# One fused attention, gating and MLP kernel: the ninth and tenth heads' q and k loads are tied to earlier heads' maxima

## The chip, the cores and the metric

The kernel runs on one core of a Trainium2 chip. The metric is the device time of one execution in microseconds (us). Lower is better.

## The reference

Four batches of eight heads (576 positions, 64 values per head) go through causal attention with a bias that comes from a running sum of `s`; its output goes through a causal convolution gate and two matrices, and then through a token mixing of rank 32 and a two-layer MLP with a residual. Cut to what matters:

```python
scores = scale * q @ k.T
bias   = -(cum[:, :, :, None] - cum[:, :, None, :])      # cum: running sum of max(s, 0)
scores = where(causal, -1e9, scores + minimum(bias, 0))
attn   = softmax(scores)                                 # row maximum, exp, row sum
x      = attn @ v                                        # heads side by side: (4, 576, 512)
gate   = sigmoid(causal 5-tap convolution of x)
x      = (gate * (x @ w_val)) @ w_out
u      = x + (x.T @ U @ V).T
out    = u + relu(u @ w_ch1) @ w_ch2
```

## The kernel before

The 32 heads (numbered 0 to 31 here, so the ninth and tenth heads are heads 8 and 9) go through one loop, `for n in range(NH + 1)`. Phase `n` of the loop writes down the scores of head `n` (`score`), the transposes of head `n - 1` (`trans`), and after each odd head the products with v for the pair (`attn_v`, `norm`). Work of the dense stages (`dense_work`) and the preparation of weights (`widen`, through `side_step`) is woven in between. From phase 8 on a finished batch's dense work is available; after the loop the rest of it and the MLP (`ch1`, `ch2`) follow.

The code doesn't fix the order in which an engine executes. Every instruction is written down with a priority (its place in the program, moved ahead by the number in `PLAN`, through the helper `Via`), and the framework plays all of them through a simulated timeline with `schedule_with_timeline_sim=True`. An instruction that has a free engine and its inputs in that timeline is placed, even if it stands many phases later in the program. The result is one fixed order per engine, in which each engine then runs: an instruction that waits holds back what stands behind it on that engine. All DMAs of this kernel are issued by SP, so SP's queue too is one such order.

Heads in `WHOLE` (0 to 7, 16 and 30) load q and k straight into the operands `Q1` and `K1`, with four extra rows that carry the bias. The other heads are split into two parts whose products sum up to more precision. For them:

- `load_raw(n)` (L276 to L282) is called two phases ahead, in phase `n - 2`. It takes a buffer with the tag `qk` (two buffers), and SP loads q into partitions 0 to 63 (L281) and k into 64 to 127 (L282). Heads 8 and 9 are the first two heads that use this tag.
- `load_head(n)` (L284) runs one phase ahead and takes `Q1` and `K1` (two buffers each) and `nm` (two buffers), the small tile in which column `c` holds the negated maxima of block `c` of the head's scores, with a sixth column for the first half of the last block. The two extra loads at L297 bring the bias rows.
- `prep_head(n)` (L304) is deferred in phase `n - 1`: `qk_hi` on ACT rounds the loaded tile into `hi`; `qk_lo` on POOL writes the remainder into `Q2`; then SP issues five copies from SBUF to SBUF: `hi` into `Q1`, `K1` and `K2` (`high`), then the remainder from `Q2` into `K2`, and last `hi` into the lower half of `Q2` (`low`). The last one overwrites what the fourth reads, so it waits until the fourth has landed. `hi`, `Q2` and `K2` have two buffers each.
- `score(n, c)` (L474) multiplies `Q1` with `K1` and `Q2` with `K2`, and DVE takes the maxima into `nm` with the same instruction that adds the mask (tag `max`). ACT then takes the exponential (`exp`), PE transposes the result (`trans`), and ACT or DVE copies it out of PSUM into `PTA` and `PTB`.

A phase's order of the blocks is one of two lists, where T is a transpose, S a score and A a product with v:

```python
ORDER0 = "T0 S0 T1 T4 S1 T3 T2 S2 S3 S4"
ORDER = "T0 T1 S0 T2 T3 S1 S2 S3 T4 S4 A0 A1"
```

`fill` adds two small matmuls of no use ahead of every group of transposes up to phase 8; in the rows they are `pt<-causal`. The entry `pace` of `PLAN` belongs to a copy in `wait_for_pace` that `PACED = False` leaves out, so in the kernel before nothing uses it. Since all instructions go through `Via`, nearly all rows below carry L132, the line of that helper; the names of the tiles tell them apart.

Of the kernel before, what the change touches and what calls it, by code (L numbers as in the profile page):

```python
# [20 lines left out]


PLAN = {
    "pace": ("gpsimd", -500),
    "qk_hi": ("scalar", 6000),
    "qk_lo": ("gpsimd", 2000),
    "put": ("sync", 3000),
# [69 lines left out]
def fused_kernel(ctx, tc, qT, kT, vP, s, wval, wout, convw, U, V, w1, w2, rows01, out):  # L97
    nc = tc.nc
    B, H, D, S = qT.shape
# [172 lines left out]
    hd = {}  # L272

    raw = {}

    def load_raw(n):  # L276

        if n < NH and n not in WHOLE:
            b, h = divmod(n, H)
            raw[n] = at.tile([P, S], F32, tag="qk", name="qk")  # L280
            nc.sync.dma_start(raw[n][0:64, :], qT[b, h])  # L281
            nc.sync.dma_start(raw[n][64:, :], kT[b, h])  # L282

# [140 lines left out]
    pace = []  # L424
# [327 lines left out]
    for n in range(NH + 1):  # L752
# [3 lines left out]
        if 2 <= n + 1 < NH:  # L756
            load_head(n + 1, n == 1)
        load_raw(n + 2)
        if n == 1:
            nc.sync.dma_start(craw.bitcast(U32), words(convw))  # L760
# [240 lines left out]
```

## Time and profile before

| | us |
|---|---|
| median of 3 runs | 765.65 |
| lowest, highest of them | 765.28, 770.79 |
| the profiled execution, its own time | 764.93 |
| its span from the first to the last instruction | 762.8 |
| PE busy, share of the span | 743.7, 98% |
| PE weight loads busy, share | 624.8, 82% |
| DVE, ACT, POOL busy | 464.4, 299.2, 291.2 |

The span is what the trace covers; 2.1 us lie around it. The engines are PE (matmul), PEld (its weight loads), DVE, ACT, POOL and SP, which only issues DMAs here. Times in rows count from the start of the span. A busy PE isn't PE at its peak, since the ends of matmuls are modelled.

### The profile page before, as it was taken

How to read it: one execution, taken by the hardware profiler on the slowest of the kernel's cores; microseconds unless marked ns; L12 is line 12 of the kernel's file. 1: busy time of each engine (PE TensorE's matmuls, PEld its weight loads, DVE VectorE, ACT ScalarE, POOL GpSimd, SP SyncE). 2: the span in 40 equal slices, each digit the busy share in tenths (PEclk: the TensorE clock that was granted, in tenths of full speed). 3: DMA queues.
4: the chain of work that ended last, by engine and by line, in shares of the span. 5: the costliest groups of instructions: out<-in, count | busy, mean ns of one | idle time of the engine just before them, and what ended most of it. 6: DMA issues, size and time to landing. Idle time of an engine off the chain costs nothing.

```text
span 762.8 us, 12349 instructions
## 1 busy us (share of the span) xinstructions
PE 743.7 (98%) x4453; PEld 624.8 (82%) x4453; DVE 464.4 (61%) x1052; ACT 299.2 (39%) x785; POOL 291.2 (38%) x321
## 2 busy tenths in 40 slices
PE   8999999899999999999899999999999999999998
PEld 4777888788887998798788888888888888888887
DVE  6798875887657755666749996424582234223234
ACT  4777756875677776633212211111121011001110
POOL 3466754553522233557197765102540024100000
PEclk9999999999999999999999999999999999999999
DMA  5734544644455432021103221100120000000023
GB/s 147 229 120 120 140 118 114 174 119 127 120 124 134 122 100 56 18 85 55 56 1 111 83 87 53 54 1 28 55 85 1 0 28 1 1 0 1 1 111 138
DMA packets 27012, 59.40 MB, mean 78 GB/s; under 512 B 4654, under 2 KB 5294, under 8 KB 26952
## 3 DMA queue, kind: packets, MB, share of 16 engines
q1 hardware_dynamic: 26952, 58.62, 26.9%
q8 instruction: 35, 0.57, 0.3%
q14 instruction: 25, 0.20, 0.1%
HBM read 37.04 MB, written 5.31 MB: 56 GB/s over the span
## 4 chain that ended last, share of the span: by engine, by line
PE 85%; DMA 4%; DVE 4%; ACT 3%; issue 2%; SPq 1%; POOL 0%; ACTq 0%; DVEq 0%
PE d L132 39%; PE acc L132 26%; PE pt L132 8%; PE av L132 6%; PE sc L132 6%; DMA qk<-in_kT 2%; DMA K<-Q 1%; DVE av L604 1%; ACT P L132 1%; DVE P L132 1%; DMA Q<-hi 1%; DVE uT L132 1%; DMA uT<-in_w 0%; ACT PTB L132 0%; ACT hi L132 0%
## 5 line engine op out<-in xcount | busy, mean ns | idle before, releaser
L132 PE MATMUL d<-u,w1h 128*128 128x512 f32 (+1 forms) x640 | 184.2, 371 | 0.0
L132 DVE SCALAR_TENSOR_TENSOR hl<-d,hh 128x512 fp32r<-128x512 f32 (+1 forms) x80 | 50.7, 635 | 170.3 <-ACT hh L861 170.3
L861 ACT ACTIVATE hh<-d 128x512 fp32r<-128x512 f32 (+1 forms) x80 | 44.2, 554 | 274.6 <-PE acc L132 149.5
L132 PEld LDWEIGHTS d<-u,w1h 128*128 128x128 f32 x640 | 116.0, 188 | 22.2
L132 PE MATMUL d<-u,w1l 128*128 128x512 f32 (+1 forms) x320 | 118.6, 371 | 0.0
L132 PE MATMUL acc<-hl,w2h 128*128 128x512 f32 (+1 forms) x320 | 105.0, 371 | 0.0
L132 PE MATMUL acc<-hh,w2h 128*128 128x512 f32 (+1 forms) x320 | 104.4, 372 | 0.5 <-DVE uT L132 0.5
L132 PE MATMUL acc<-hh,w2l 128*128 128x512 f32 (+1 forms) x320 | 102.0, 371 | 0.0
L132 ACT ACTIVATE P<-P,nm 64x64 f32<-64x64 f32 (+4 forms) x160 | 89.0, 560 | 25.2 <-DVE nm L132 24.6
L132 PE MATMUL sc<-K,Q 68*128 68x288 f32 (+11 forms) x384 | 89.1, 344 | 4.6 <-ACT PTB L132 1.8
L132 DVE CUSTOM_DVE_ANT_0 P<-sc,causal 64x64 f32<-64x64 f32 (+4 forms) x160 | 65.2, 421 | 30.8 <-PE sc L132 28.2
L132 PE MATMUL pt<-ident,P 128*128 128x128 f32 x480 | 78.5, 284 | 5.4 <-ACT PTA L139 2.6
L132 DVE TENSOR_TENSOR uT<-acc,uT 128x512 f32<-128x512 f32 (+1 forms) x120 | 70.1, 630 | 22.3 <-PE acc L132 22.2
L132 PEld LDWEIGHTS sc<-K,Q 68*128 68x128 f32 (+2 forms) x384 | 62.2, 193 | 13.2 <-ACT PTB L132 2.6
L132 PEld LDWEIGHTS d<-u,w1l 128*128 128x128 f32 x320 | 60.2, 188 | 11.0
L132 PEld LDWEIGHTS acc<-hh,w2h 128*128 128x128 f32 x320 | 58.7, 188 | 12.1 <-issue 0.9
L132 PEld LDWEIGHTS acc<-hl,w2h 128*128 128x128 f32 x320 | 58.8, 188 | 11.2
L132 PEld LDWEIGHTS acc<-hh,w2l 128*128 128x128 f32 x320 | 58.6, 188 | 11.3
L132 PEld LDWEIGHTS pt<-ident,P 128*128 128x128 f32 x480 | 56.3, 145 | 12.3 <-ACT PTA L139 3.6
L604 DVE SCALAR_TENSOR_TENSOR av<-X,cw,av 128x576 f32<-128x576 f32 x64 | 52.3, 817 | 4.9 <-ACT av L132 4.5
L132 DVE SCALAR_TENSOR_TENSOR scr<-raw,scr 128x512 uint32<-128x512 uint32 (+1 forms) x56 | 52.4, 936 | 1.4
L132 DVE TENSOR_SCALAR scr<-scr 128x512 uint32<-128x512 uint32 x56 | 43.3, 773 | 11.9 <-POOL w1l L132 6.3
(123 smaller groups left out, 1286.9 us busy)
## 6 DMA issues: line engine op xcount, KB each, us to landing
raw<-in_w SPq DMA_DIRECT2D x28, 512.0 KB
K<-hi SPq DMA_DIRECT2D x44, 144.0 KB
Q<-hi SPq DMA_DIRECT2D x44, 144.0 KB
V<-in_vP SPq DMA_DIRECT2D x16, 320.0 KB
out<-uT SPq DMA_DIRECT2D x16, 256.0 KB
qk<-in_qT SPq DMA_DIRECT2D x22, 144.0 KB
qk<-in_kT SPq DMA_DIRECT2D x22, 144.0 KB
K<-Q SPq DMA_DIRECT2D x22, 144.0 KB
```

The source lines that it names most:

```text
L132: return f(*args, **kw)
L604: Via("tap").scalar_tensor_tensor(g, X[:, k:k + S], cw[:, p, k:k + 1], g, op0=ALU.mult, op1=ALU.add,)
L861: Via("hh").activation(h_, o, AF.Relu)
```

## The change

Ahead of the two loads of heads 8 and 9 a copy of one column, by POOL, is put into the first column of the tile that is about to be loaded. Its source is column 4 of `nm` of the head three before: head 5 for head 8, head 6 for head 9. Column 4 is the last of that head's maxima. The loads overwrite that column, so the framework lets them wait for the copy, and the copy for the maxima. The values computed are the same. `pace` gets a 0 in place of -500, so that the copy keeps its place in the program as its priority.

```diff
 PLAN = {
-    "pace": ("gpsimd", -500),
+    "pace": ("gpsimd", 0),
...
             raw[n] = at.tile([P, S], F32, tag="qk", name="qk")
+            if H <= n < H + 2:
+
+                Via("pace").tensor_copy(raw[n][:, 0:1], hd[n - 3]["nm"][:, 4:5])
             nc.sync.dma_start(raw[n][0:64, :], qT[b, h])
             nc.sync.dma_start(raw[n][64:, :], kT[b, h])
```

## Rows read from the trace of the kernel before

**Rows 1.** The page's part 1: busy time, share of the span and instructions.

```profile
PE 743.7 (98%) x4453; PEld 624.8 (82%) x4453; DVE 464.4 (61%) x1052; ACT 299.2 (39%) x785; POOL 291.2 (38%) x321
```

**Rows 2.** Windows: stretch, its length, busy time per engine, PE clock, DMA share, GB/s.

```profile
12.00:16.00 4.00, 3.53 (x16) 3.02 (x17) 0.59 (x4) 2.46 (x10) 0.26 (x1) 0.57 0.93 218
16.00:17.00 1.00, 1.00 (x12) 0.98 (x11) 0.00 (x0) 0.97 (x3) 0.00 (x0) 1.00 0.92 260
23.00:57.00 34.00, 34.00 (x252) 25.78 (x252) 30.07 (x92) 26.49 (x80) 19.56 (x22) 1.00 0.57 169
57.00:70.00 13.00, 12.64 (x98) 9.70 (x95) 9.94 (x24) 8.66 (x26) 9.44 (x9) 1.00 0.42 131
90.00:130.00 40.00, 37.92 (x288) 33.93 (x289) 26.88 (x83) 25.59 (x74) 20.38 (x27) 0.96 0.46 116
130.00:323.00 193.00, 186.61 (x1419) 161.48 (x1419) 140.31 (x418) 137.28 (x397) 79.89 (x89) 0.99 0.43 108
```

**Rows 3.** The timeline of PE: start, duration, operation; in brackets idle before and releaser.

```profile
12.47 0.60 PE L132 MATMUL sc<-K,Q 68*128 68x64 f32 x2 [0.98 <-DVE nm L132]
...
22.47 0.66 PE L132 MATMUL pt<-ident,P 128*128 128x128 f32 x4 [0.69 <-ACT P L132]
...
66.37 2.53 PE L132 MATMUL sc<-K,Q 68*128 68x320 f32 x8 [0.17 <-ACT PTA L132]
...
69.42 0.39 PE L132 MATMUL sc<-K,Q 68*128 68x64 f32 x2
70.17 0.38 PE L132 MATMUL pt<-causal 128*128 128x256 bf16 x2 [0.36 <-DVE nm L132]
...
76.95 0.41 PE L132 MATMUL sc<-K,Q 68*128 68x64 f32 x2
```

**Rows 4.** The timeline of SP, the queue that issues the DMAs.

```profile
4.99 0.47 SPq L281 DMA_DIRECT2D qk<-in_qT  x1
5.50 0.59 SPq L282 DMA_DIRECT2D qk<-in_kT  x1
...
17.00 0.50 SPq L132 DMA_DIRECT2D Q<-hi  x1
...
18.21 0.49 SPq L282 DMA_DIRECT2D qk<-in_kT  x1
```

**Rows 5.** The timeline of ACT, the `hi` of heads 9 and 10.

```profile
21.08 0.68 ACT L132 ACTIVATE hi<-qk 128x576 fp32r<-128x576 f32 x1 [1.72 <-DMA qk<-in_kT]
...
65.04 0.69 ACT L132 ACTIVATE hi<-qk 128x576 fp32r<-128x576 f32 x1 [3.19 <-DMA Q<-hi]
```

**Rows 6.** The tile `qk`: instructions, count, duration least/median/most in ns, first and last start.

```profile
L132 ACT ACTIVATE hi<-qk x22: 665/684/690, 10.1 to 271.5; 128x576 fp32r<-128x576 f32 x22
L132 POOL TENSOR_TENSOR Q<-qk,hi x22: 1402/1430/1902, 10.9 to 284.0; 128x576 fp32r<-128x576 f32 x22
```

**Rows 7.** The timeline of DVE, the last maxima of heads 5 and 6.

```profile
54.57 0.09 DVE L132 DVE_READ_ACCUMULATOR2_ANT nm<- 128x1 f32 x1
...
60.04 0.08 DVE L132 DVE_READ_ACCUMULATOR2_ANT nm<- 128x1 f32 x1
```

**Rows 8.** The timeline of POOL.

```profile
23.33 0.20 POOL L365 TENSOR_SCALAR uT<-uT 128x20 f32<-128x20 f32 x1
...
55.94 0.62 POOL L132 TENSOR_SCALAR wvh<-uT 128x512 fp32r<-128x512 f32 x1 [2.53 <-DVE uT L132]
...
59.00 1.27 POOL L132 TENSOR_TENSOR wvl<-uT 128x512 fp32r<-128x512 f32 x1 [0.69 <-DVE rs L132]
```

**Rows 9.** The chain of waits: start, duration, what; DMAs from issue to landing.

```profile
12.81 4.17 DMA K<-Q
...
59.47 4.74 DMA Q<-hi
...
127.25 3.40 DMA qk<-in_kT
...
170.89 2.31 DMA K<-Q
...
239.96 1.99 DMA qk<-in_kT
```

## The prediction, made before the changed kernel ran

> **What bounds the kernel now.** I read the busy shares first, then windows by stage, then the chain of waits, and then the timelines of PE, SP, ACT, POOL and DVE around the places where the chain leaves PE. PE is busy for 98% of the span [rows 1], so what a change can give is PE idle time, or time at a low clock. The windows show where that is. From 23 to 57 us PE has no idle time at all [rows 2]: whatever comes out of the stretch before 23 us is carried through, and whatever is added on another engine there costs nothing as long as PE's inputs arrive. Before it stands a start-up with PE idle time and with four microseconds at a mean granted clock of 0.57 [rows 2], between the levels of 1.2 and 2.4 GHz. From 57 to 70 us PE is idle for 0.36 us of 13, and from 90 to 323 us for (40 - 37.92) + (193 - 186.61) = 8.47 us [rows 2].
>
> The chain of waits is the third thing to see. Between 12.8 and 22.5 us it doesn't run through PE at all, but through work of heads 8 and 9, which PE needs only at 69.42 and 76.95 us (their first scores) [rows 3]. Their loads stand at 5 us in SP's order, since nothing holds them back [rows 4], and the scheduler has placed `hi`, `lo` and three of the five copies of each behind them. The last copy of head 8 stands at 17.00 us in SP's order because it waits for the fourth, which takes 4.17 us to land [rows 4, 9]; head 9's load of k, behind it in SP's order, starts at 18.21 us [rows 4]; ACT, whose next instruction is head 9's `hi`, stands still for 1.72 us until that lands [rows 5]; an exponential behind it comes late, and PE idles for 0.69 us ahead of its transposes at 22.47 us [rows 3].
>
> A second such place is at 65 us: ACT stands still for 3.19 us, since head 10's `hi` has to wait until head 8's copy of `hi` into `Q1`, issued at 59.47 us, has landed 4.74 us later [rows 5, 9]. PE loses 0.17 and 0.36 us behind it [rows 3].
>
> **The change part by part.**
>
> *The two copies.* The trace has no POOL copy of one column. Its nearest small row on POOL is 128 x 20 in 0.20 us [rows 8]; I take that, twice, and nothing as the lower bound. Head 5's last maxima are there at 54.57 + 0.09 = 54.66 us, head 6's at 60.04 + 0.08 = 60.12 us [rows 7]. At the first of these times POOL is idle (2.53 us ahead of 55.94), at the second it is in an instruction until 60.27 [rows 8]. The cover is that idle time; without it, the copy would hold back weight preparation by 0.2 us, which no chain here ends in. Cost: 0.
>
> *What leaves the start.* Two `hi` of 0.68 us on ACT, two `lo` of 1.43 us on POOL [rows 6], four loads, six copies, and the loads of heads 10 and 11, which follow in the freed buffers. PE gets back the 0.69 us at 22.47 us, and carries it to about 65 us, as PE has no idle time in which it could be lost [rows 2, 3]. Gain: 0.69, bounds 0.3 and 0.69. The slow clock from 12 to 16 us costs 4 x (1 - 0.57) = 1.72 us of PE time [rows 2]. It follows on a PE that idled 0.98 us ahead of head 1's first scores at 12.47 us, and a little before that [rows 3]; these wait for the cumulated bias, not for head 8. So I take 0 of it, and keep 0 and 1.72 as bounds.
>
> *Where it goes.* Into 55 to 75 us. POOL there gets 2 x 1.43 + 2 x 0.20 = 3.3 us onto the 9.44 of 13 us that it is busy, ACT 1.4 us onto 8.66, and the DMA engines ten transfers of 147 KB, 1.47 MB, which over 13 us are 113 GB/s onto 131 [rows 2, 6]. That is 244 GB/s, where the trace has 218 at a share of 0.93 in the crowded stretch from 12 to 16 us [rows 2]. So everything fits, and nothing has much room.
>
> *Head 8, just in time or late.* From 54.66 us: copy 0.20, first issue 0.47, and from 55.4 us on the load of k, which lands after 1.99 to 3.40 us [rows 4, 9], so at 57.4 to 58.8. `hi` 0.69 and `lo` 1.43 [rows 6], the latter behind up to 1.27 us of other POOL work [rows 8]: 59.5 to 62.2. The fourth copy takes 2.31 to 4.17 us [rows 9]: 61.8 to 66.4. The fifth, which waits for it, takes as much as the fourth at best and 4.74 us at most [rows 9]: 64.1 to 71.1. PE asks at 69.42 [rows 3], or at 68.7 if the 0.69 us is carried. So head 8 is 4.6 us early or 2.4 us late; the middle, 67.6, is early, so I take 0, with 2.4 us as the upper bound.
>
> What the trace says of such a transfer: 4.17 and 4.74 us in crowded stretches, 2.31 in a quiet one [rows 9]. The Trainium skill, "DMA: Bandwidth & Descriptors", section "Anatomy of one DMA — SWDGE (gpsimd) path", gives a fit, for POOL-issued DMAs, of about 2.0 us plus the bytes at 436 GB/s; as an estimate from that page 147 KB would take 2.3 us each. By that, head 8 is ready at about 65 us and never late; by the crowded rows it is late. The two rows in question are twice the fit, so this case's crowded stretches don't agree with it.
>
> *Head 9* waits for 60.12 us. The same terms (POOL in its instruction until 60.27, then copy, load, `hi`, `lo`, two copies in a row) give 70.2 to 77.2 us against 76.95 - 0.69 = 76.3. But its loads share SP with head 8's fifth copy, which holds SP until head 8's fourth has landed, 66.4 us at the latest. In the worst order head 9 is 5.9 us later still, so 6.9 us late.
>
> *The stall at 65 us* (0.53 us of PE): head 10's `hi` still waits for copies of head 8's `hi`, now later, and head 9's `hi` joins it. I take it as moved, not removed: 0, bounds -0.53 and +0.7 (one more stall of the size of that at 22.47 us).
>
> **Sum.** 764.93 (the profiled execution's own time) - 0.69 + 0 + 0 + 0 = 764.2. That execution is 0.72 below the median of the runs, so in terms of the median: 764.9. With the bounds of the small terms the likeliest case alone lies between 763 and 766.5.
>
> **The rivals.**
>
> *A, late operands (slower).* Heads 8 and 9 miss PE's order. Price: up to 2.4 us for head 8 and 6.9 for head 9, and for each such idle time a stretch at half clock like that from 12 to 16 us, 1.72 us; at most 12.7 us, 777.6. The middle, head 8 late by 1.2 us with one slow stretch, gives 764.9 + 2.9 = 767.8. It decides against the change as soon as the lateness is over 0.69 us, and by over 1% only if head 9's loads fall behind head 8's fifth copy on SP. For it: SP's order is one, the transfers of 4.17 and 4.74 us [rows 9]. Against: the scheduler knows of these waits and can put other matmuls ahead of those scores. The clock is part of this price. The trace has it at 0.57 after PE had idled [rows 2, 3]; the Trainium skill, "TensorE: Matmul & The Clock Gate", section "HAM oscillation — how this bites in real kernels", says the same of a PE that waits for a DMA: it falls back to the half clock and does the work behind the wait cold. On that the trace agrees.
>
> *B, the whole start comes free.* The slow clock goes too, and the stall at 65 us: 764.9 - 1.72 - 0.53 = 762.7. For it: six copies and two loads fewer in the stretch of 0.93 DMA share [rows 2]. Against: head 1's scores don't wait for them.
>
> *C, another order later on.* The schedule is played through anew, and shifts of a microsecond at 20 to 75 us can change which instruction comes first for the rest of the attention. At stake is the idle time from 90 to 323 us, 8.47 us: gone, 756.4; doubled, 773.4. Nothing in the trace says which.
>
> *D, no stall at stake:* PE's 0.69 us comes back as another wait before 65 us. Then 765.65, inside the likeliest case's own range.
>
> **How the numbers follow.** The likeliest case with D 0.48; A 0.27, of which 0.10 beyond 1%; B 0.12; C 0.13, of which 0.07 over 1% faster and 0.03 over 1% slower. One per cent, 7.7 us, is about what a measurement of this kernel can tell from no change. So faster 0.07, slower 0.13, same 0.80. The range leaves out most of C's faster part and the far end of A and of C's slower part, together below 0.2: 760.0 to 770.5.
>
> **What would show it.** Right: no `hi` on ACT before 55 us, SP's first load of `qk` at about 55 us, PE without idle time at 22 us, head 1's first scores unmoved at about 12.5 us, head 5's last maxima about 0.7 us earlier. Wrong, for A: PE waiting on `K<-Q`, `Q<-hi` or the first two-part scores between 65 and 80 us, or a granted clock below 1 there. For B: a clock of 1 from 12 to 16 us. For C: stages up to 90 us alike and the difference behind them. What would make the forecast wrong most easily is SP's order around 60 us.

## The result and the profile after

The changed kernel is slower by about half a per cent. Its median is 772.64 us (770.87 to 775.61, 18 runs); the kernel before, run beside it, has 767.44 us (764.36 to 772.53, 18 runs). The ratio is 1.0058 with a 95% interval of 1.0038 to 1.0078 (it isn't the quotient of the two medians, which is 1.0068). The prediction was 764.9 us, within 760.0 and 770.5: the time lies above that range, and the sign is the other one. The size is within the 1% that the prediction called "same". The profiled execution of the changed kernel took 772.69 us, 7.8 us more than that of before, so the two traces differ by more than the medians do (5.2 us).

The first part of the page shows that the work has stayed what it was [rows 1]: 2 more instructions on POOL, the copies, and busy times within 1% of before. The added time is time in which PE waits or runs slowly.

```profile
PE 745.4 (97%) x4453; PEld 626.8 (81%) x4453; DVE 461.5 (60%) x1052; ACT 299.1 (39%) x785; POOL 291.1 (38%) x323
```

Windows of the kernel after, with the columns of [rows 2] (stretch, length, busy time of PE, PEld, DVE, ACT and POOL, granted PE clock, DMA share, GB/s):

```profile
12.00:20.00 8.00, 6.43 (x29) 5.79 (x30) 0.59 (x4) 3.67 (x13) 0.00 (x0) 0.57 0.63 179
20.00:57.00 37.00, 36.74 (x270) 28.63 (x269) 29.48 (x94) 27.59 (x82) 18.70 (x21) 1.00 0.41 128
57.00:70.00 13.00, 13.00 (x97) 9.53 (x96) 9.81 (x28) 9.06 (x27) 8.53 (x10) 1.00 0.55 137
70.00:90.00 20.00, 16.51 (x124) 14.12 (x123) 14.11 (x43) 13.57 (x40) 11.79 (x11) 0.91 0.71 188
90.00:130.00 40.00, 37.46 (x289) 33.11 (x289) 32.16 (x89) 26.97 (x78) 22.74 (x26) 1.00 0.52 124
130.00:150.00 20.00, 19.13 (x156) 16.88 (x152) 14.23 (x45) 15.13 (x45) 10.82 (x14) 1.00 0.54 144
150.00:160.00 10.00, 7.59 (x55) 6.43 (x53) 9.97 (x31) 8.99 (x26) 6.25 (x8) 1.00 0.66 171
160.00:310.00 150.00, 145.58 (x1114) 127.60 (x1115) 101.46 (x319) 103.93 (x305) 56.12 (x64) 1.00 0.46 113
310.00:330.00 20.00, 18.53 (x131) 14.76 (x131) 13.47 (x36) 12.02 (x32) 10.75 (x11) 0.91 0.06 17
```

The same windows of the kernel before, without the two that [rows 2] has already:

```profile
12.00:20.00 8.00, 7.53 (x40) 6.14 (x41) 2.13 (x11) 5.26 (x17) 0.26 (x1) 0.79 0.75 182
20.00:57.00 37.00, 36.31 (x270) 27.75 (x270) 30.80 (x96) 28.41 (x85) 20.72 (x22) 1.00 0.59 177
...
70.00:90.00 20.00, 19.51 (x154) 16.65 (x153) 18.75 (x56) 16.18 (x47) 14.03 (x13) 1.00 0.60 150
...
130.00:150.00 20.00, 19.80 (x153) 16.96 (x151) 16.87 (x50) 17.37 (x49) 11.12 (x13) 1.00 0.54 142
150.00:160.00 10.00, 7.83 (x44) 6.04 (x44) 9.13 (x26) 6.90 (x21) 4.22 (x6) 0.83 0.49 120
160.00:310.00 150.00, 147.44 (x1143) 129.51 (x1143) 103.66 (x318) 104.98 (x308) 55.79 (x64) 1.00 0.44 112
310.00:330.00 20.00, 18.53 (x141) 15.84 (x140) 14.70 (x33) 9.79 (x26) 12.77 (x12) 1.00 0.08 27
```

Lost PE time in a window can be counted as its length less PE's busy time, plus its length times one less the clock. From 12 to 20 us that is 0.47 + 8 x 0.21 = 2.15 us before and 1.57 + 8 x 0.43 = 5.01 after. All windows in that way:

| stretch, us | lost before | lost after | difference |
|---|---|---|---|
| 12 to 20 | 2.15 | 5.01 | +2.86 |
| 20 to 57 | 0.69 | 0.26 | -0.43 |
| 57 to 70 | 0.36 | 0.00 | -0.36 |
| 70 to 90 | 0.49 | 5.29 | +4.80 |
| 90 to 130 | 3.68 | 2.54 | -1.14 |
| 130 to 160 | 4.07 | 3.28 | -0.79 |
| 160 to 310 | 2.56 | 4.42 | +1.86 |
| 310 to 330 | 1.47 | 3.27 | +1.80 |

The sum is +8.6 for a span that is 7.9 us longer. The same work doesn't stand in the same window in both, and idle time at a low clock is counted twice (0.7 us of the 5.01), so each entry is good to about a microsecond. Two entries are the largest: the start and the stretch from 70 to 90 us. In between the change gives what it was to give, the idle time at 22 us and at 65 us. A large part of the entry at the start will turn out to belong to the one execution and not to the kernel (e2 and e16 below).

**The start.** SP's order of the kernel before (start, duration, line, operation), with the stores `ef<-uT` of bias rows behind both of head 1's loads of bias rows:

```profile
9.57 0.69 SPq L297 DMA_DIRECT2D K<-uT  x1
10.37 0.61 SPq L297 DMA_DIRECT2D Q<-uT  x1
...
11.65 1.06 SPq L341 DMA_DIRECT2D ef<-uT  x2
```

SP's order of the kernel after:

```profile
9.56 0.69 SPq L300 DMA_DIRECT2D K<-uT  x1
10.30 0.43 SPq L344 DMA_DIRECT2D ef<-uT  x1
10.84 0.63 SPq L300 DMA_DIRECT2D Q<-uT  x1
...
56.54 0.47 SPq L284 DMA_DIRECT2D qk<-in_qT  x1
...
65.68 0.46 SPq L132 DMA_DIRECT2D Q<-hi  x1
66.19 0.60 SPq L285 DMA_DIRECT2D qk<-in_kT  x1
...
68.28 0.59 SPq L285 DMA_DIRECT2D qk<-in_kT  x1
```

One store has moved ahead of head 1's second load, which is issued 0.47 us later; from there to head 1's first scores it takes 2.73 us and not 2.10. The timeline of PE after, with idle time and releaser in brackets, shows head 1's first scores at 13.57 us and not at 12.47 [rows 3]:

```profile
13.57 0.66 PE L132 MATMUL sc<-K,Q 68*128 68x64 f32 x2 [2.66 <-issue]
...
71.56 0.39 PE L132 MATMUL sc<-K,Q 68*128 68x64 f32 x2
74.48 0.52 PE L132 MATMUL pt<-causal 128*128 128x256 bf16 x2 [2.53 <-ACT PTA L139]
```

**The stall at 72 us.** The last row of that timeline is the largest single wait of PE between 20 and 90 us, and its releaser is ACT. The timeline of ACT after:

```profile
73.09 0.68 ACT L132 ACTIVATE hi<-qk 128x576 fp32r<-128x576 f32 x1 [1.94 <-DMA qk<-in_kT]
73.68 0.55 ACT L132 ACTIVATE P<-P,nm 128x320 f32<-128x320 f32 x1
74.22 0.20 ACT L139 ACTIVATE PTA<-pt 128x64 f32<-128x64 f32 x1
```

ACT stands in front of head 10's `hi` until that head's load of k, issued at 68.28 us, has landed. Behind it in ACT's order are an exponential of head 7 and the copy out of PSUM that PE needs. PE idles for 2.53 us and then works at a reduced clock: the window from 70 to 90 us has 0.91 in the mean.

### The profile page after: what moved, and what is told of

The parts are those of the page before. It is cut to its first block, busy times and chain, and to the rows that moved or that the text cites. A ratio compares the mean times of both kernels' runs of the same rounds, so it can differ in the third digit from the quotient of the medians.

```text
span 770.7 us, 12346 instructions
## 1 busy us (share of the span) xinstructions
PE 745.4 (97%) x4453; PEld 626.8 (81%) x4453; DVE 461.5 (60%) x1052; ACT 299.1 (39%) x785; POOL 291.1 (38%) x323
## 4 chain that ended last, share of the span: by engine, by line
PE 80%; DMA 6%; DVE 5%; ACT 3%; issue 2%; SPq 2%; POOL 1%; ACTq 0%; POOLq 0%; DVEq 0%
PE d L132 37%; PE acc L132 26%; PE pt L132 7%; PE av L132 5%; PE sc L132 5%; DMA qk<-in_kT 3%; DMA K<-Q 2%; DVE av L607 2%; DVE P L132 1%; SPq L132 1%; DVE uT L132 1%; ACT P L132 1%; POOL Q L132 1%; ACT hi L132 1%; DMA Q<-hi 1%
```

## The experiments

Each kernel was compared with the kernel before on the same chip; a ratio is to that kernel, with its 95% interval. The diffs are against the kernel after. Beside the times, the traces were compared by one event: the start of each head's first maxima on DVE, against the same event of before. The shifts, in us:

| kernel | head 1 | 2 | 8 | 9 | 10 | 17 | 31 | ratio |
|---|---|---|---|---|---|---|---|---|
| after | +1.16 | +2.56 | +2.34 | +4.93 | +6.74 | +6.26 | +6.29 | 1.0058 |
| store held (e1) | +0.05 | +1.51 | +1.34 | +3.72 | +5.09 | +9.03 | +8.81 | 1.0035 |
| two heads earlier (e4) | +0.90 | +1.10 | +1.89 | +0.50 | +4.04 | +0.76 | +2.40 | 1.0016 |
| head 10 too (e5) | +1.14 | +2.57 | +2.22 | +0.48 | +2.04 | +6.84 | +6.22 | 0.9982 |
| warm (e7) | +2.32 | +0.92 | -0.14 | +2.30 | +4.17 | +4.91 | +6.49 | 1.0054 |
| only head 8 (e2) | +1.15 | +1.08 | +0.88 | +4.14 | +6.92 | +6.07 | +6.35 | 1.0078 |
| only head 9 (e3) | +1.16 | +2.10 | +1.31 | -0.36 | +6.03 | +6.63 | +7.31 | 1.0086 |
| e5 and e1 (e11) | -0.21 | +0.16 | -0.12 | -1.79 | -0.31 | +0.90 | +0.60 | 0.9997 |
| only head 10 (e13) | +0.05 | +1.09 | -0.51 | -1.28 | -0.48 | +0.98 | +1.18 | 0.9970 |
| `hi` of head 10 on POOL (e16) | +0.89 | +1.10 | +1.09 | +0.17 | +6.05 | +4.70 | +4.66 | 1.0074 |
| only heads 10, 11 (e17) | -0.21 | -0.01 | -0.86 | -1.63 | -1.08 | -1.27 | -1.59 | 0.9978 |

A shift is of one execution, the ratio of many: the execution of e5 in the table is the slowest of its ten.

My theory after the two traces was that two things cost the time, a store that slipped ahead of head 1's second load, and ACT standing in front of head 10's `hi`. Its rivals were late operands of heads 8 and 9 (A of the prediction), the half clock at the start by itself, and an order later on that went worse (C).

### The store at the start

e1 puts a write into a tile that the stores read, so that they are placed later.

```diff
     load_head(1, True)
+    nc.gpsimd.memset(F[3][:, 0:1], 1.0)
     for i in range(2):
         nc.sync.dma_start(ef[:, i], EF[i])
```

> The changed kernel with one more POOL memset (a column of ones, written a second time), so that the store of the bias rows that went ahead of head 1's second bias load on SP can only go behind it. Theory S, the start costs: head 1's first scores come at 12.5 us instead of 13.57, PE's stretch at half clock gets shorter, head 2's first maxima come 1.2 to 2.6 us earlier than in the changed kernel, and the time falls by 1.2 to 2.6 us, to about 770 to 771. Rival L, all of the loss is made where heads 8 to 10 are prepared (70 to 80 us): the time stays at 772 to 773, what the start gives being lost there.

769.61 us (765.89 to 773.75, 10 runs) beside 768.01, ratio 1.0035 (1.0012 to 1.0059). SP has its old order again and head 1 is back in its place (+0.05). Up to head 9 the trace keeps 1.0 to 1.2 us of that. So the cause of head 1's delay is shown. That the total gains is not: the intervals of e1 and after overlap, and the trace loses more at 150 to 180 us than it had gained. The stall at 72 us is there as in after: PE idles for 2.34 us ahead of 73.28.

e7 leaves SP's order at the start and puts 18 small matmuls of no use ahead of head 1's first scores, to hold PE's clock up.

```diff
             o = ps[:, 0:k1 - k0]
+            if n == 1 and c == 0:
+                fill(ps, 18)
             if n in WHOLE:
```

> The changed kernel with 18 more small matmuls of no use ahead of head 1's first scores, in the time in which PE idles from 10.9 to 13.6 us. Theory C, half of what the start costs is the half clock that follows on this idle time (13.4 to 19.9 us in the changed kernel): the granted clock stays at 1 from 12 to 20 us, head 2's first maxima come about 3 us earlier, and the time falls by 2 to 3 us, to about 770. Rival: the clock falls in any case, or ACT and DVE bound that stretch, and the time stays at 772 to 773.

772.15 us (770.16 to 774.90, 8 runs) beside 768.01, ratio 1.0054 (1.0027 to 1.0080). The clock is 1.00 from 12 to 20 us in place of 0.57, and head 8 comes 0.14 us early instead of 2.34 late. Nothing of it is left at the end: between heads 8 and 10 the shift grows by 4.3 us, as it does in after (4.4). ACT stands in front of head 10's `hi` for 1.64 us here too. So a clean start alone doesn't bring the time back.

How long the clock stays low at the start isn't settled by the order. Until 20 us, e2 and e16 issue the same stores and loads on SP as after, give PE the same order of work, and let it wait for 2.65 us ahead of head 1's first scores, where after has 2.66. Yet head 2 is 2.56 us late in after and 1.08 and 1.10 in e2 and e16. The window of e2:

```profile
12.00:20.00 8.00, 6.43 (x34) 5.32 (x35) 1.20 (x7) 4.43 (x16) 0.20 (x1) 0.79 0.62 168
```

PE is busy for 6.43 us as in after, at a clock of 0.79 and not 0.57; before has 0.79 too. So of head 2's delay in after about 1.1 us belongs to the kernel, and 1.5 us to its profiled execution.

### Head 8, head 9, or the next one

e2 and e3 hold back one of the two heads alone.

```diff
-            if H <= n < H + 2:
+            if n == H:
```

> The changed kernel with the copy for head 8 alone: head 9's loads wait for nothing of their own and follow head 8's on SP. Theory Q (ACT in front of a hi whose load lands late costs PE's idle 2.5 us at 72 us): head 9's and then head 10's loads come earlier and outside the crowd, PE's idle time at 72 us falls below 1 us, the start is as in the changed kernel, and the time falls by 2 to 4 us, to about 769 to 770. Rival: holding head 8 is what costs, and the time stays at 772 to 773.

773.71 us (771.07 to 775.80, 5 runs) beside 766.89, ratio 1.0078 (1.0050 to 1.0106). The timeline of ACT in e2:

```profile
71.20 0.68 ACT L132 ACTIVATE hi<-qk 128x576 fp32r<-128x576 f32 x1 [3.68 <-DMA qk<-in_kT]
```

And the timeline of PE in e2:

```profile
72.58 0.59 PE L132 MATMUL pt<-causal 128*128 128x256 bf16 x2 [2.79 <-ACT PTA L139]
```

Head 9's loads go out at 56 and 57 us here, eight to nine microseconds earlier than in after, and its `hi` runs at 61.46 us. Yet the stall is at least as long, and again in front of head 10's `hi`. Rival A, with head 9 as the late one, falls by this.

```diff
-            if H <= n < H + 2:
+            if n == H + 1:
```

> The changed kernel with the copy for head 9 alone: head 8 is loaded and prepared at the start, as in the kernel before, head 9 is held until head 6's maxima. Theory S and Q: the start still has one store ahead of head 1's second bias load, so head 1's scores come about 1 us late (13.5 us) and the half clock follows; head 10's load stands early, so PE doesn't idle for 2.5 us at 72 us. Together 1 to 3 us over the kernel before, 768 to 770. Rival: it is the 1 us of head 9's lateness alone that makes the loss, and the time is as in the changed kernel, 772 to 773.

773.72 us (772.18 to 775.12, 4 runs) beside 766.89, ratio 1.0086 (1.0053 to 1.0120). Head 9 comes 0.36 us early, and head 10 6.03 us late: ACT now stands for 2.46 us in front of the `hi` at 86.24 us, and PE for 1.85 us ahead of 87.47. The two halves don't add up to the whole. Each by itself costs as much as both. In both traces ACT stands in front of a `hi`; in e2 that is for head 10's load, while the row of e3 names a load of U that SP issued at 83.94 us, right behind a load of k at 83.23, so what e3's `hi` waited for is less sure.

e5 does the opposite and holds back head 10 as well, behind the maxima of head 7.

```diff
-            if H <= n < H + 2:
+            if H <= n < H + 3:
```

> The changed kernel with head 10's loads tied in the same way, to head 7's last maxima. Theory Q, PE's idle 2.5 us at 72 to 74.5 us comes from ACT, which stands in front of head 10's hi while that head's load of k lands, and not from late operands of heads 8 and 9: with the load held, the scheduler places that hi further behind, the exponentials of head 7 go ahead of it, the idle time goes or falls below 1 us, and the time falls by 2 to 4 us, to about 769 to 771. Rival O, head 8's own operands are late: the idle time stays ahead of head 8's scores and the time at 772 to 773 or more.

767.17 us (764.83 to 772.47, 10 runs) beside 768.01, ratio 0.9982 (0.9954 to 1.0011), whose interval lies below that of after. The window of e5 in the stretch of the stall:

```profile
70.00:90.00 20.00, 19.47 (x154) 16.44 (x153) 17.61 (x54) 16.11 (x48) 14.49 (x15) 1.00 0.74 194
```

Against 16.51 busy at 0.91 in after, PE is busy for 19.47 us at full clock, and head 9 is 0.48 us late instead of 4.93. Until head 8 the two kernels run alike (+2.22 and +2.34). One wait has been moved, in front of a load that is now issued at 74.97 us and later, and the loss from 70 to 90 us is gone. Of the runs this speaks most clearly for the cause. A larger share of DMA time by itself can't have been it: the share rose from 0.71 to 0.74. Two things stay open. The table's execution of e5 loses what it had gained further on: head 16 is 1.22 us late, head 17 again 6.84. The window between them:

```profile
150.00:160.00 10.00, 5.15 (x21) 4.05 (x20) 6.71 (x22) 6.21 (x19) 2.81 (x4) 0.66 0.54 143
```

So that the gain reaches the end rests on the medians, and the faster executions have no profile. And the ratios of e5 and after lie 0.76% apart, 5.8 us, with intervals of 0.2 to 0.3% to either side; the 3 to 5 us by which the traces differ from head 9 to head 16 fit into that, without being measured by it.

e4 keeps the change but lets both loads go two phases earlier, behind heads 3 and 4.

```diff
-                Via("pace").tensor_copy(raw[n][:, 0:1], hd[n - 3]["nm"][:, 4:5])
+                Via("pace").tensor_copy(raw[n][:, 0:1], hd[n - 5]["nm"][:, 4:5])
...
-        load_raw(n + 2)
+        if n not in (H - 2, H - 1):
+            load_raw(n + 2)
+        if n in (H - 4, H - 3):
+            load_raw(n + 4)
```

> The changed kernel with the loads of heads 8 and 9 called two phases earlier and tied to the last maxima of heads 3 and 4 instead of 5 and 6, so that they still stay out of the start but come at about 40 and 46 us. Theory L, the preparation of heads 8 to 10 comes too late and too crowded: PE's idle 2.5 us at 72 to 74.5 us and the half clock behind it go, the time falls by 3 to 5 us, to about 768 to 769. Rival S, the start alone costs: the start is as in the changed kernel, and so is the time, 772 to 773.

769.99 us (767.09 to 774.71, 10 runs) beside 768.01, ratio 1.0016 (0.9986 to 1.0045). Between after and no change, and its interval touches both. Head 9 is in time (+0.50): the buffers come free earlier, head 10's loads go out at 51.91 us in place of 67.72, and ACT stands for only 0.70 us in front of its `hi`.

### Where the stall goes when its engine is changed

e16 has the SP order of after, but gives head 10's `hi` to POOL, so that ACT has nothing to wait for.

```diff
-            lambda: rnd("qk_hi", hi, t["qk"]),
+            lambda: rnd("xh" if n == H + 2 else "qk_hi", hi, t["qk"]),
```

> The changed kernel with head 10's hi, and no other, computed by POOL in place of ACT; SP's order of DMAs is the same as in the changed kernel, so head 10's load of k lands as late as there. Theory Q (ACT standing in front of that hi makes PE's idle 2.5 us at 72 us and the half clock behind it): the exponentials behind it go ahead, the idle time falls below 1 us, head 9's and 10's maxima come 3 to 4 us earlier than in the changed kernel, and the time falls by 3 to 4 us, to about 768 to 769.5. Rival O (the operands or the crowd of DMAs themselves): idle time and time stay, 772 to 773.

772.61 us (769.52 to 776.82, 12 runs) beside 766.56, ratio 1.0074 (1.0050 to 1.0099). The stall at 72 us is gone and head 9 comes at +0.17, so it was that one instruction on ACT that held PE. But the time is not back, though 3 to 4 us less were expected. The timeline of ACT in e16:

```profile
79.87 0.68 ACT L132 ACTIVATE hi<-qk 128x576 fp32r<-128x576 f32 x1 [2.58 <-DMA qk<-in_qT]
```

And the timeline of PE in e16:

```profile
80.88 3.68 PE L132 MATMUL av<-PTB,V 128*64 128x192 f32 x20 [2.27 <-ACT PTB L132]
```

ACT stands in front of head 11's `hi` instead, and the same chain follows 8 us later.

### The stall in the kernel before

e13 undoes the change for heads 8 and 9 and holds back head 10 alone, whose `hi` is the place of the stall at 65 us [rows 5].

```diff
-            if H <= n < H + 2:
+            if n == H + 2:
```

> The kernel before with head 10's loads alone held, until head 7's last maxima; heads 8 and 9 are loaded and prepared at the start. Theory Q says that ACT's 3.2 us in front of head 10's hi at 65 us goes, and PE's 0.5 us behind it, at most 1 us in all: the time is that of the kernel before within 1.5 us. Rival: head 10's early place is worth the whole gain that holding it brought to the changed kernel, and the time falls by 3 us or more.

765.02 us (760.99 to 768.82, 10 runs) beside 766.89, ratio 0.9970 (0.9945 to 0.9995). This version is faster than both kernels, by little: its interval only just leaves out 1. The timeline of ACT in e13 shows the held `hi` ten microseconds later and without idle time ahead of it:

```profile
75.57 0.68 ACT L132 ACTIVATE hi<-qk 128x576 fp32r<-128x576 f32 x1
```

e17 holds back head 11 as well.

```diff
-            if H <= n < H + 2:
+            if H + 2 <= n < H + 4:
```

> The kernel before with heads 10 and 11 held until the last maxima of heads 7 and 8, heads 8 and 9 left at the start. If holding what ACT stands in front of is what pays, it is at least as fast as holding head 10 alone, 763 to 765.5. Rival: the order later on decides, and it lies within 2 us of the kernel before on either side.

764.30 us (762.17 to 769.96, 10 runs) beside 766.56, ratio 0.9978 (0.9946 to 1.0011): as good as e13 as far as can be told.

e11 joins e5 and e1, to see whether the two causes add.

```diff
-            if H <= n < H + 2:
+            if H <= n < H + 3:
...
+    nc.gpsimd.memset(F[3][:, 0:1], 1.0)
     for i in range(2):
```

> Heads 8, 9 and 10 held, and the store of the bias rows held behind head 1's second bias load, so both edits that helped alone. If the two losses are apart (start: 1.2 us; ACT's wait at 72 us: 4 us), it is 1 to 2 us below the kernel with heads 8 to 10 held, so 0.3 to 0.5% below the kernel before: 764 to 766. Rival: the order later on is drawn anew and takes it back, 767 to 770.

766.81 us (763.62 to 771.24, 12 runs) beside 766.89, ratio 0.9997 (0.9976 to 1.0018). In the trace the heads of the table up to 10 are at most 0.16 us late, most of them early. Of the 2.41 us that head 2 gains over e5, e1 explains 1.05 by the store; the rest goes with a clock of 0.79 from 12 to 20 us, where both e5 and e1 had 0.57. In the time, e11 can't be told from e5 nor from before. What the start costs at the end stays open by that.

### Two attempts to warm the start

The fillers of e7 on the kernel before (e8) and on e13 (e18).

> The kernel before with the 18 small matmuls alone. The granted clock stays at 1 from 12 to 16 us and head 2's first maxima come 1 to 1.7 us earlier. If that is carried to the end, 1 to 1.7 us below the kernel before; if ACT's wait in front of head 10's hi at 65 us and the dense stage behind it set the pace, the time of the kernel before within 1 us.

> The kernel before with head 10's loads alone held and with 18 small matmuls of no use ahead of head 1's first scores. If the half clock at the start costs what the windows show (1.7 us) and it is carried, 762.5 to 764; if it is lost behind head 8, as it was when only the fillers were added to the changed kernel, 764.5 to 766.

Both were misses. e8: 776.49 us (773.84 to 779.01, 4 runs) beside 766.56, ratio 1.0122 (1.0076 to 1.0167). e18: 774.81 us (769.95 to 777.20, 10 runs), ratio 1.0090 (1.0060 to 1.0119). Both traces lose 6.6 us by head 3. The timeline of ACT in e8:

```profile
20.88 0.68 ACT L132 ACTIVATE hi<-qk 128x576 fp32r<-128x576 f32 x1 [4.10 <-DMA qk<-in_kT]
```

The timeline of PE in e8:

```profile
21.99 0.58 PE L132 MATMUL sc<-K,Q 68*128 68x64 f32 x2 [2.81 <-ACT PTA L132]
```

A window of e8:

```profile
20.00:30.00 10.00, 6.71 (x22) 4.64 (x23) 2.32 (x14) 6.45 (x20) 2.95 (x4) 0.61 0.89 253
```

Head 9's load lands when it did before: its `hi` starts at 20.88 us, before at 21.08 [rows 5]. But the new order has put that `hi` ahead of work that ACT could have done, and it stands for 4.10 us in place of 1.72. So the same instruction with the same load costs PE 0.69 us in one order and 2.81 us with a slow stretch behind it in another. (A second wait of this kind follows in e8: ACT stands for 1.55 us ahead of 23.48 until a load of the convolution's weights has landed, and PE idles for 1.31 us.) The price lies in what stands behind the waiting instruction, not in the load.

## Why the prediction was wrong, point by point

**The two copies: right in size, not in place.** The timeline of POOL after:

```profile
56.12 0.19 POOL L283 COPY qk<-nm 128x1 f32<-128x1 f32 x1 [0.86 <-DVE nm L132]
...
61.73 1.41 POOL L132 TENSOR_TENSOR Q<-qk,hi 128x576 fp32r<-128x576 f32 x1
63.10 1.26 POOL L132 TENSOR_TENSOR wvl<-uT 128x512 fp32r<-128x512 f32 x1
64.31 0.17 POOL L283 COPY qk<-nm 128x1 f32<-128x1 f32 x1
```

0.19 and 0.17 us, where 0.20 was taken from the 128 x 20 row [rows 8]. The first comes 1.4 us later than the step had it, since head 5 does. The second comes 4.2 us later: head 6's last maxima are there at 61.67 us, 1.6 us later than before, and then the copy stands for 2.6 us behind head 8's `lo` and a piece of weight preparation. The step asked what the copy would hold back on POOL, not what POOL would hold back: head 9's load of q goes out at 64.51 us, right behind the copy. By e2 this wasn't what cost the time.

**What leaves the start: the gain right, the rest of the step wrong.** The stall at 22.47 us is gone; from 20 to 57 us PE's idle time falls from 0.69 to 0.26 us. The sentence that failed is that head 1's first scores "wait for the cumulated bias, not for head 8" and so stay at 12.5 us. They do not wait for head 8, but the order in which SP issues their bias rows is drawn anew when head 8's transfers leave SP, and one store went ahead of the second of them (e1 shows it). The idle time that this adds, 1.1 us, was in no term. The term for the slow clock, taken as 0 with a gain as its only other bound, came out as a loss in the profiled execution: 0.57 over 8 us in place of 0.79, 1.8 us. A bound on that side was missing; but e2 and e16, with the same start, had 0.79, so this part is the execution's. Head 5's last maxima, which were to come 0.7 us earlier, come 1.4 us later.

**Where it goes: fits in throughput, not in time of landing.** The stretch from 57 to 70 us moved 137 GB/s at a share of 0.55, less than the 244 worked out, because head 9's work came later than 70 us; from there to 90 us it is 188 GB/s at 0.71. No engine became the bound. Some of the transfers that stand together there took long: head 10's load of k was issued at 68.28 us and released ACT at 73.09, 4.8 us later, where two transfers of before took 1.99 and 2.31 [rows 9]. The step on head 8 called the short ones quiet and the long ones crowded. No row says so, and the trace of before doesn't separate them in that way: the DMA share was 0.78 over the 2.31 us from 170.89 us and 0.76 over the 4.74 us from 59.47. What makes such a transfer long stays open.

**Head 8: right.** Its fourth copy stands in the chain of waits of after (start, duration, what), as does head 9's:

```profile
63.32 2.34 DMA K<-Q
...
71.37 4.88 DMA K<-Q
```

Head 8's lies within the 2.31 to 4.17 of the step; the fifth, which waits for it, was issued at 65.68 us, and the scores at 71.56 waited for neither. The Trainium skill's fit for POOL-issued DMAs ("DMA: Bandwidth & Descriptors", section "Anatomy of one DMA — SWDGE (gpsimd) path") gives, as an estimate for 147 KB, 2.3 us; head 8's copy, issued by SP, agrees, and head 9's at 4.88 us took twice that, as the two long rows of before had.

**Head 9: its condition came true, its price didn't.** Its load of k was issued at 66.19 us, behind head 8's fifth copy at 65.68. Its last copy went out at 76.31 us and its scores started at 82.01. I had priced this as PE waiting for those scores. By e2, where head 9's loads go eight microseconds earlier and the stall is as long, PE was not waiting for them. The sum was off as well: head 8's terms, counted from 60.27 us, give 69.7 to 76.7 us and not 70.2 to 77.2; only the upper end of rival A hangs on that.

**The stall at 65 us: the step that failed most.** It was "moved, not removed", as I wrote, and then priced at 0 with +0.7 as the upper bound, the size of the stall at 22.47 us. It came back as 2.53 us of PE idle time and, with the slow clock, 4.8 us lost from 70 to 90 us. What was overlooked is what it waits for. I had head 10's `hi` wait for copies that free its buffer. It waits for head 10's own load, which the change had pushed behind those of heads 8 and 9 in SP's order. The moved loads were followed to their own consumers, and not to the loads behind them on the queue. For the size, the row of ACT's 3.19 us of waiting [rows 5] was the place to start: the kernel before lost only 0.53 us of PE behind it, but e8 shows 4.10 us of waiting on ACT turn into 2.81 on PE. It is no upper bound either: in after 1.94 us on ACT became 2.53 on PE, since PE also waits for the `hi` itself and the exponential ahead of its copy.

**Rival A** had the place (PE idle and a low clock between 65 and 80 us) and a price of 2.9 us, where that window lost 4.8. Its mechanism, operands that come late, is not what happened, so the place was luck; of its two signs the low clock came true and the wait for operands did not. The part about the clock held: PE idles for 2.53 us and the clock from 70 to 90 us falls to 0.91. That agrees with the Trainium skill, "TensorE: Matmul & The Clock Gate", section "HAM oscillation — how this bites in real kernels", which has the work behind a wait run cold. It isn't so each time: e7's execution has 2.57 us of idle time in that window and a clock of 1.00.

**Rival B** didn't happen; the slow clock grew in the profiled execution. **Rival C** can't be excluded for the part behind 90 us: the entries there are +1.86 and -1.93 with +1.80 at the end. But what e5 removes stands before 90 us.

**The sum.** -0.69 was to be all of it. In the ledger the gains of 0.43 and 0.36 us are there; against them stand +2.86 at the start, of which 1.8 in the clock's term and 1.1 in none, and +4.80 in the term of the stall at 65 us, taken as 0 with +0.7 as its bound. The bounds of the small terms (763 to 766.5) were too narrow by the second alone. A minor part is the median: before gives 767.44 us over 18 runs, where the three shown gave 765.65.

**Left open.** How much of the loss at the start reaches the end: e1 and e11 show it in the trace, and neither shows it in the time. How much of the time the stall explains: e5 and e16 show that it can be taken away, but e2, e3 and e16 were expected to be faster by it and weren't, each with another wait of ACT and PE in its trace. Each edit draws the order anew, and e16, which moves a single `hi`, meets the next stall; so another order later on (C) isn't excluded as a part of the loss. Why the store slipped ahead lies in the scheduler's timeline, which no trace shows.

## What to carry to other kernels

A load that is held back is to be followed in three directions: to its consumer, to what stands behind it on the queue that it leaves and on the one that it enters, and to the in-order engine that will stand in front of the next load. Price a wait of such an engine by what is queued behind it: 1.9 us of waiting on ACT became 2.5 us on PE here, and 4.1 us became 2.8. If one wait is to be added, this case speaks for the load whose consumer already stalls (head 10, ratio 0.9970, with an interval that only just leaves out 1), and against loads that were merely early.

## What the runs showed of the hardware that was not expected

**The same idle time with and without a slow clock.** At the end of the attention, the timeline of PE in the kernel before has these three waits:

```profile
313.75 0.85 PE L132 MATMUL pt<-ident,P 128*128 128x128 f32 x5 [0.31 <-ACT PTA L139]
...
315.31 0.66 PE L132 MATMUL pt<-ident,P 128*128 128x128 f32 x4 [0.15 <-ACT P L132]
...
316.92 0.40 PE L132 MATMUL d<-V4h,ast 128*128 128x288 f32 x1 [0.94 <-DVE ast L148]
```

In the kernel after they are the same, 6.3 us later:

```profile
320.04 0.85 PE L132 MATMUL pt<-ident,P 128*128 128x128 f32 x5 [0.32 <-ACT PTA L139]
...
321.60 0.66 PE L132 MATMUL pt<-ident,P 128*128 128x128 f32 x4 [0.15 <-ACT P L132]
...
323.21 0.40 PE L132 MATMUL d<-V4h,ast 128*128 128x288 f32 x1 [0.94 <-DVE ast L148]
```

PE is busy for 18.53 us of the 20 in both, yet the clock granted from 310 to 330 us was 1.00 before and 0.91 after, which is 1.8 us. Head 31's maxima are 6.29 us late, the matrices behind them about 8.0. So this part of the longer span of after isn't explained by the order at all. The execution of e17 has the reverse at 150 us, where that of before had 0.83 with 2.17 us of idle time ahead of 152.50. The timeline of PE in e17:

```profile
151.57 0.44 PE L132 MATMUL pt<-ident,P 128*128 128x128 f32 x2 [2.92 <-ACT PTA L139]
```

The window of e17:

```profile
150.00:160.00 10.00, 7.43 (x49) 5.79 (x50) 9.36 (x26) 7.87 (x23) 4.48 (x6) 1.00 0.46 119
```

More idle time, and no slow clock. The start is a third case: e2 and after with the same wait, at 0.79 and 0.57. What decides is open. It bears on how far one execution can be trusted: the runs of before lie between 764.36 and 772.53 us, and e5, whose profile is 6.2 us late at head 31, has a median below that of before.
